# Cutting the last weight load of a decode kernel into five pieces instead of four

## The chip, the cores and the metric

One core of one Trainium2 chip. The metric is device time in microseconds (us). Before the change the kernel takes 1273.3 us (median of 3 runs, 1273.01 to 1273.58). Beside the time each run records the span of the core, about 2 us shorter.

## The reference, cut to what matters

A gated mix of a decode attention block and a small dense block. Two batch rows, one new token, 8 key/value heads, 32768 cached positions of 256 values, all bf16.

```python
def reference(A_x, A_k_cache, A_v_cache, A_wq, A_wo, B_x, B_w1, B_b1, B_w2, B_b2, gate_w):
    x = A_x                                             # [2, 1, 448]
    g = _sigmoid((x * gate_w).sum(-1, keepdims=True))
    a = _A_ref(x, A_k_cache, A_v_cache, A_wq, A_wo)     # softmax(q k) v, then @ wo [4096, 448]
    b = _B_ref(x, B_w1, B_b1, B_w2, B_b2)               # gelu(x w1 + b1) w2 + b2
    return g * a + (1 - g) * b
```

The two caches are 537 MB; each byte is used once. `wo` is 3.7 MB and is the last thing to be loaded.

## The kernel before

A ring of three buffers streams K and V. At the end of the queue of loads stand, in this order, the last V (three pieces), W2 and WO, all on one queue of the sync engine (SP). WO is laid out with 32 column blocks of 448 values in each of 128 partitions; a block is 112 KB. `WOP` says where WO is cut; each piece has its own semaphore.

```python
    NC = HD // P                          # 32 column blocks
    WOP = (0, 16, 28, 31, 32)             # pieces of 16, 12, 3 and 1 blocks
    ...                                   # --- cut ---
                elif kind == "WO":        # sync engine, L378 to L383
                    src = A_wo.rearrange("(p c) n -> p (c n)", p=P)
                    for i in range(len(WOP) - 1):
                        c0, c1 = WOP[i] * Dm, WOP[i + 1] * Dm
                        dma(lambda e, ...: e.dma_start(wo_v[:, c0:c1], src[:, c0:c1]), f"pW{i}", ("wo", i))
    ...                                   # --- cut ---
            def FIN(i):                   # TensorE: the product with WO, L551
                E.wait(f"pW{i}", ("wo", i))
                for c in range(WOP[i], WOP[i + 1]):
                    for q in range(2):
                        E.ins(lambda e, c=c, q=q: e.matmul(
                            ps_a[64 * q:64 * q + Bn, :], attnT[:, c:Bn * NC:NC],
                            wo_v[:, c * Dm + q * DQ:c * Dm + (q + 1) * DQ], ...))
    ...                                   # --- cut: the end of TensorE's program ---
            TT()
            do_FB()                       # the product with W2, 28 matmuls, L459
            E.wait("dve", "at")
            for i in range(len(WOP) - 1):
                FIN(i)                    # two matmuls a block, 64 in all
```

After the last matmul VectorE and ScalarE each cast one half of the result (L793, L656), and SP stores it (L396).

Of the kernel before, what the change touches and what calls it, by code (L numbers as in the profile page):

```python
# [125 lines left out]
def bass_gated_mix__gqa_block_cached__dense_activation_gelu__decode_kernel(  # L126
# [53 lines left out]
    assert (NTILES - LAG) % UNIT == 0  # L180
    PIECES = (64, 32, 32)
    NC = HD // P
    WOP = (0, 16, 28, 31, 32)
    DQ = Dm // 2
    GELU_C = 0.7978845608028654
    GELU_A = 0.044715
# [7 lines left out]
    for i in range(len(PIECES)):  # L194
        sch.stream(f"pV{i}", 16)
    for i in range(len(WOP) - 1):
        sch.stream(f"pW{i}", 16)
# [3 lines left out]
    with contextlib.ExitStack() as es:  # L201
# [157 lines left out]
        def prog_sp(E):  # L359
            def dma(fn, stream, key):  # L360
                E.ins(fn, key=key, stream=stream)

            for d in order:
# [15 lines left out]
                elif kind == "WO":  # L379
# [3 lines that stand above are left out]
                        dma(lambda e, src=src, c0=c0, c1=c1: e.dma_start(wo_v[:, c0:c1], src[:, c0:c1]), f"pW{i}", ("wo", i))  # L383
# [15 lines left out]
        def prog_pe(E):  # L399
# [147 lines left out]
            def FIN(i):  # L547
# [5 lines that stand above are left out]
                            wo_v[:, c * Dm + q * DQ:c * Dm + (q + 1) * DQ], start=False, stop=(c == NC - 1),  # L553
                            skip_group_check=True), key=("FIN" if (c == NC - 1 and q == 1) else None))
# [39 lines left out]
            E.wait("dve", "at")  # L594
            for i in range(len(WOP) - 1):
                FIN(i)
# [245 lines left out]
```

## Time and profile before

| what | value | where |
|---|---|---|
| span of the core | 1271.6 us | page |
| DMA busy | 90% or more in 39 of 40 slices, 431 GB/s | page |
| TensorE (PE), VectorE (DVE) busy | 55%, 54% | page |
| last WO piece landed | 1268.97 us | semaphore records of the trace |
| PE's last matmul ends | 1269.60 us | trace |

Lines of the page of the kernel before: span; busy time of the engines; the DMA share in 40 slices, in tenths; the chain of work that ended last, by engine.

```profile
span 1271.6 us, 8088 instructions
...
PE 698.9 (55%) x4544; PEld 146.0 (11%) x2016; DVE 685.8 (54%) x528; ACT 43.7 (3%) x183; POOL 3.3 (0%) x14
...
DMA  9999999999999999999999999999999999999998
...
DMA 63%; DVE 21%; PE 13%; issue 3%; SPq 0%; another core or an unknown queue 0%
```

The DMA row is 9 everywhere but in the last slice: the kernel is a stream. This change touches only the stream's very end, so what it can win lies there. That is the tail, from 1226 us. Here it is in the timeline of the kernel before. Columns: start (us), duration (us), engine, line, operation, destination <- source, shape, count, and in brackets the idle time before it and what ended it.

```profile
1226.42 1.84 SPq L383 DMA_DIRECT2D ring<-in_A_wo_dram  x4
...
1262.09 2.78 PE L459 MATMUL ps_f<-ring,hT_bf 128*2 128x224 bf16 x28
...
1264.76 2.14 PE L551 MATMUL ps_f<-ring,attnT 128*2 128x224 bf16 x32
...
1267.90 1.70 PE L551 MATMUL ps_f<-ring,attnT 128*2 128x224 bf16 x32 [1.00 <-DMA ring<-in_A_wo_dram]
...
1269.64 0.38 DVE L793 CAST pexp<-ps_f 2x224 bf16<-2x224 f32 x1 [7.21 <-PE ps_f L551]
```

SP issues the four WO loads by 1228.3 us, 40 us ahead. PE does the W2 product (28 matmuls), the 32 matmuls of piece 0, idles 1.00 us, and does all 32 others in one unbroken run of 1.70 us. The bracket names a WO load once: after piece 1 nothing made PE wait.

The issue table of the kernel before: size of each load, and us from its issue to its landing.

```profile
ring<-in_A_wo_dram SPq DMA_DIRECT2D x1, 1792.0 KB, 38.2
...
ring<-in_A_wo_dram SPq DMA_DIRECT2D x1, 1344.0 KB, 41.0
ring<-in_A_wo_dram SPq DMA_DIRECT2D x1, 336.0 KB, 41.3
ring<-in_A_wo_dram SPq DMA_DIRECT2D x1, 112.0 KB, 41.1
```

Issued at 1226.42, 1226.89, 1227.36 and 1227.83 us, they landed at 1264.6, 1267.9, 1268.7 and 1269.0. Twelve blocks took 3.2 us more, three 0.8, one 0.3: the DMA engine that finishes last brings a block about every 0.27 us (16 blocks in 4.34 us). Stretches of 2 us of the kernel before show that the others finish sooner. Columns: stretch; its length; busy time and count of each engine; granted clock; DMA share; GB/s.

```profile
core 0: us, PE busy (x) PEld busy (x) DVE busy (x) ACT busy (x) POOL busy (x), PEclk, DMA share, GB/s
...
1264.00:1266.00 2.00, 2.00 (x28) 1.29 (x26) 0.00 (x0) 0.00 (x0) 0.00 (x0) 0.58 0.96 401
1266.00:1268.00 2.00, 1.00 (x24) 0.69 (x20) 0.00 (x0) 0.00 (x0) 0.00 (x0) 1.00 0.53 204
1268.00:1270.00 2.00, 1.60 (x32) 1.23 (x28) 0.36 (x1) 0.34 (x1) 0.00 (x0) 1.00 0.02 6
```

The DMA share falls to 0.53 and 0.02 while the slower engines work on. The clock, 0.5 for most of the tail, is full from 1265.7 us.

### The profile page before, as it was taken

The numbers are of one execution on the slowest core, as the hardware profiler recorded it, in microseconds if no ns is written. First come the engines' busy times: TensorE is split into PE (matmuls) and PEld (weight loads), VectorE is DVE, ScalarE is ACT, GpSimd is POOL, SyncE is SP. The second block draws the span as 40 slices with busy tenths as digits, with TensorE's granted clock in tenths as the row PEclk, the third lists the DMA queues.
The fourth block names the chain that finished last, engine by engine and source line by source line (L and its number), as shares of the span: only waits on it lengthen the run. The fifth ranks groups of instructions, "written<-read, shape, count | busy, mean of one in ns | idle before, by whom it ended". The sixth has DMA issues, their size and how long they took to land.

```text
span 1271.6 us, 8088 instructions
## 1 busy us (share of the span) xinstructions
PE 698.9 (55%) x4544; PEld 146.0 (11%) x2016; DVE 685.8 (54%) x528; ACT 43.7 (3%) x183; POOL 3.3 (0%) x14
## 2 busy tenths in 40 slices
PE   4566566644466443665544665455664437655465
PEld 3111011100011100111100111000110001111012
DVE  2875537655365563556735466453755636566341
ACT  1000000000000000000000000000000000000000
POOL 1000000000000000000000000000000000000000
PEclk9988788767887777887778887778876778877686
DMA  9999999999999999999999999999999999999998
GB/s 404 441 434 431 429 429 435 431 439 434 431 429 435 437 431 437 435 431 429 433 439 431 437 435 429 431 433 439 431 437 433 431 431 433 439 431 433 437 423 359
DMA packets 10971, 547.59 MB, mean 431 GB/s; under 512 B 1352, under 2 KB 1616, under 8 KB 1872
## 3 DMA queue, kind: packets, MB, share of 16 engines
q1 hardware_dynamic: 10804, 547.43, 99.6%
q8 instruction: 8, 0.13, 0.0%
q10 hardware_dynamic: 156, 0.01, 0.0%
q14 instruction: 3, 0.02, 0.0%
HBM read 547.43 MB, written 0.00 MB: 431 GB/s over the span
## 4 chain that ended last, share of the span: by engine, by line
DMA 63%; DVE 21%; PE 13%; issue 3%; SPq 0%; another core or an unknown queue 0%
DMA ring<-in_A_k_cache_dram 60%; DVE ring L722 19%; PE ps_o L335 4%; PE ps_s L490 3%; PE ps_s L335 3%; DMA ring<-in_A_wo_dram 3%; DVE mx L726 1%; PE ps_o L539 1%; PE ps_m L499 0%; PE ps_m L504 0%; DVE gmax L728 0%; DVE gmx L732 0%; PE ps_f L551 0%; SPq L376 0%
## 5 line engine op out<-in xcount | busy, mean ns | idle before, releaser
L722 DVE STREAM_TRANSPOSE ring<-ring 128x2048 uint32<-128x2048 uint32 x256 | 565.2, 2275 | 390.2 <-DMA ring<-in_A_k_cache_dram 389.9
L490 PE MATMUL ps_s<-ring,Abd 128*128 128x512 bf16 x1024 | 427.0, 417 | 428.7 <-DVE ring L722 428.3
L335 PE MATMUL ps_s<-ring,Abd 128*128 128x512 bf16 x1024 | 423.3, 413 | 0.0
L490 PEld LDWEIGHTS ps_s<-ring,Abd 128*128 128x128 bf16 x1024 | 106.1, 104 | 852.0 <-DVE ring L722 480.1
L335 PE MATMUL ps_o<-ring,PT 128*24 128x512 bf16 x1504 | 112.9, 408 | 0.0
L539 PE MATMUL ps_o<-ring,PT 128*24 128x512 bf16 x544 | 58.1, 427 | 12.6 <-DMA ring<-in_A_v_cache_dram 12.6
L509 PE MATMUL ps_f<-o_sb,selg 128*32 128x257 f32 x32 | 17.0, 634 | 83.5 <-DVE o_sb L763 83.5
L763 DVE SCALAR_TENSOR_TENSOR o_sb<-ps_o,mask,o_sb 128x256 f32<-128x256 f32 x112 | 54.1, 483 | 8.9 <-PE ps_o L539 5.0
L726 DVE TENSOR_REDUCE mx<-ps_s 128x1 f32<-128x1024 f32 x16 | 19.6, 1224 | 59.9 <-PE ps_s L335 59.9
L636 ACT ACTIVATE negm<-ps_m 128x1 f32<-128x1 f32 x16 | 2.7, 171 | 1156.4 <-PE ps_m L504 1156.4
L739 DVE STREAM_TRANSPOSE PT<-pexp 128x1024 bf16<-128x1024 bf16 x16 | 19.9, 1245 | 36.8 <-PE ps_o L335 36.8
L539 PEld LDWEIGHTS ps_o<-ring,PT 128*24 128x24 bf16 x544 | 14.7, 100 | 104.1 <-issue 86.9
L736 DVE COPY ls<-lsum 128x1 f32<-128x1 f32 x16 | 2.5, 154 | 31.8 <-ACT pexp L640 31.8
L630 ACT COPY Abd<-qrep 32x16 bf16 (+1 forms) x128 | 19.4, 199 | 0.6
L640 ACT ACTIVATE pexp<-ps_s,negm 128x1024 bf16<-128x1024 f32 x16 | 17.8, 1113 | 1.7
L499 PE MATMUL ps_m<-ident_f,mx 128*1 128x128 f32 x32 | 6.1, 271 | 21.1 <-DVE mx L726 21.1
L760 DVE TENSOR_SCALAR o_sb<-ps_o,mask 128x256 f32<-128x256 f32 x16 | 7.6, 475 | 17.7 <-PE ps_o L335 17.7
L509 PEld LDWEIGHTS ps_f<-o_sb,selg 128*32 128x32 f32 x32 | 2.9, 139 | 101.6 <-DVE o_sb L763 99.5
L504 PE MATMUL ps_m<-ones_f,gmx 1*128 1x1 f32 x32 | 6.0, 256 | 9.9 <-DVE gmx L732 9.9
L728 DVE TENSOR_REDUCE gmax<-ps_m 1x2 f32<-1x128 f32 x16 | 4.5, 279 | 7.5 <-PE ps_m L499 7.5
L420 PE MATMUL ps_s<-xT,ring 128*128 128x2 bf16 x128 | 3.6, 165 | 8.1 <-DMA ring<-in_A_wq_dram 8.1
L504 PEld LDWEIGHTS ps_m<-ones_f,gmx 1*128 1x128 f32 x32 | 4.7, 183 | 14.6 <-DVE gmx L732 14.6
(76 smaller groups left out, 64.1 us busy)
## 6 DMA issues: line engine op xcount, KB each, us to landing
ring<-in_A_v_cache_dram SPq DMA_DIRECT2D x1, 4096.0 KB, 27.0
ring<-in_A_v_cache_dram SPq DMA_DIRECT2D x2, 2048.0 KB, 33.7
ring<-in_A_wq_dram SPq DMA_DIRECT2D x1, 3072.0 KB, 10.5
ring<-in_A_wo_dram SPq DMA_DIRECT2D x1, 1792.0 KB, 38.2
ring<-in_B_w_dram SPq DMA_DIRECT2D x1, 1568.0 KB, 34.3
ring<-in_B_w_dram SPq DMA_DIRECT2D x1, 1344.0 KB, 13.6
ring<-in_A_wo_dram SPq DMA_DIRECT2D x1, 1344.0 KB, 41.0
ring<-in_A_wq_dram SPq DMA_DIRECT2D x1, 512.0 KB, 11.3
```

What stands on the lines that cost most here:

```text
L335: return e.add_instruction(mybir.InstMatmult(name=f"I-{nc.next_id()}", engine=mybir.EngineType.PE, ldweights=False, ins=[e.lower_ap(x), e. ...
L490: fn = lambda e, o=o, x=x, st=st, sp=sp, s=s, w=w: e.matmul(o, a_win(s, w), x, start=st, stop=sp, skip_group_check=True)
L504: E.ins(lambda e: e.matmul(ps_m[:, C_BC:C_BC + 1], gmx[:, :], ones_f[0:1, 0:1], start=True, stop=True), key=("M2", g))
L509: E.ins(lambda e: e.matmul(ps_oa, selg[:, :], o_sb[:, :], start=False, stop=False, skip_group_check=True), key=("OT", g))
L539: fn = lambda e, o=o, x=x, wt=wt, st=st, sp=sp, j=j: e.matmul(o, wt, x, start=st, stop=sp, skip_group_check=True)
L630: E.ins(lambda e, o=o, Q=Q, c=c: e.copy(o[:, :, c:c + 2], qrep[32 * Q:32 * Q + 32, :, bass.ds(E.dyn(2 * g, 2), 2)]), key=(("A", g) if (Q = ...
L640: E.ins(lambda e: e.activation(pexp[:, :].rearrange("p (r i a) -> p i r a", r=CR, i=2), ps_s[:, :].rearrange("p (i r a) -> p i r a", i=2, ...
L722: E.ins(lambda e: e.transpose(k_words(idx, blk), k_words(idx, blk)), key=("T", idx, blk))
L726: E.ins(lambda e: e.tensor_reduce(mx[:, :], ps_s[:, :], AX.X, ALU.max), key=("MX", g))
L739: E.ins(lambda e: e.transpose(PT[:, :], pexp[:, :]), key=("PT", g))
L760: E.ins(lambda e, p=p, m=m: e.tensor_scalar(o_sb[:, 0:Dh], p, m, None, op0=ALU.mult), key=("OS0", g))
L763: E.ins(lambda e, p=p, m=m: e.scalar_tensor_tensor(out=o_sb[:, 0:Dh], in0=p, scalar=m, in1=o_sb[:, 0:Dh], op0=ALU.mult, op1=ALU.add), key= ...
```

## The change

The intent: less work for PE behind the last landings. A cut at 14, 23 and 28 instead of 16 and 28 lets PE finish 14 more matmuls before block 28 is there.

```diff
-    WOP = (0, 16, 28, 31, 32)
+    WOP = (0, 14, 23, 28, 31, 32)
```

It adds one DMA, one semaphore and one wait.

## The prediction

> **What bounds the kernel now.** The page of the profile: the 16 DMA engines are 90% busy or more in 39 of 40 slices, 547 MB at 431 GB/s over 1271.6 us; PE is busy 55%, DVE 54%. The chain of waits is 63% DMA. The change touches only the last loads, so only the tail after 1226 us can move.
>
> **The tail now** (timeline and chain of waits from 1220 us). The four WO loads are issued at about 1226.4, 1226.9, 1227.4 and 1227.8 us, behind a backlog of about 40 us, so issuing costs nothing. By the issue table they land 38.2, 41.0, 41.3 and 41.1 us later: about 1264.6, 1267.85, 1268.7 and 1268.95. The differences (12 column blocks in 3.25 us, 3 in 0.8, 1 in 0.27) say that the DMA engine that finishes last brings a block in about 0.27 us. Most engines are done earlier: by stretch, the DMA share falls from 1.0 at 1264 to 0.33 at 1267-1268 and 0.04 at 1268-1269.
> PE ends the W2 product at about 1264.7 and does the 32 matmuls of piece 0 by 1266.9, at a clock that goes from 0.50 to 1.00 near 1265.6. It idles 1.0 us for piece 1, until 1267.9. Then 32 matmuls (24, 6, 2) follow without a gap, 1.70 us, to 1269.62. So pieces 2 and 3 have landed before PE asks for them: behind the landing of block 28, PE is the limit, not the DMA. Only two casts (0.38 us) and the store follow.
>
> **What the change does.** It removes nothing: same bytes, same 64 WO matmuls, same engines. It adds one DMA issue on SP (0.43 us, hidden by the backlog), one semaphore, one wait on PE, and one more completion per DMA engine. With 0.27 us per block[...]:
> - piece 0 (14 blocks) lands at about 1264.1, before PE ends W2: no wait; 28 matmuls end near 1266.5.
> - piece 1 (to block 23) at about 1266.5: hardly a wait; 18 matmuls, done by 1267.4 at full clock.
> - piece 2 (to 28) at about 1267.9, as now: 10 matmuls, done by 1268.45.
> - piece 3 (to 31) at about 1268.7: now a real wait of about 0.3 us; 6 matmuls, 0.3 us.
> - piece 4 at about 1269.0: 2 matmuls; the end at 1269.3.
> So 14 matmuls less lie behind block 28's landing, and the limit becomes the landing of the last block. Of the 14 x 0.045 = 0.65 us moved off, about 0.3 us is gain; the rest becomes waiting for pieces 3 and 4. On 1273 us that is 0.02%, less than the spread of three runs (0.57 us).
>
> The Trainium skill, "DMA: Bandwidth & Descriptors", section "Anatomy of one DMA", gives a fixed cost of about 2 us per DMA that is mostly completion latency; in this trace queued pieces land 0.27 us apart, so it overlaps and must not be charged again.
>
> **Time:** 1273.0 us, 8 in 10 between 1271.9 and 1274.2. Faster by over 2%: 0.3%; within 2%: 99.4%; slower by over 2%: 0.3%.
>
> **What would show it.** All before 1226 us unchanged. PE's idle in front of the WO product in more, shorter parts; after the last landing 2 to 4 matmuls instead of some 20; the end about 0.3 us earlier relative to the last landing.
>
> **What would make it wrong.** If the half clock lasts through the tail, a matmul costs about 0.085 us and the gain is gone. If the slowest engine loses over 0.3 us to the extra piece, it is slower by some tenths. If runs differ by 0.1% anyway, only the trace shows the sign.

## The result, and the profile after

| | before | after |
|---|---|---|
| time, median (6 runs each) | 1273.10 us | 1272.85 us |
| lowest to highest | 1272.99 to 1273.58 | 1272.63 to 1273.11 |
| W2 landed to last WO landed (trace) | 8.64 us | 8.63 us |
| last WO landed to PE's end (trace) | 0.63 us | 0.33 us |
| W2 landed to PE's end (trace) | 9.26 us | 8.96 us |

The ratio is 0.9998, with a 95% interval of 0.9985 to 1.001. A ratio here is the mean time of one kernel's fast runs over that of the other's of the same rounds, so not quite the ratio of the medians. The verdict is "same". The time lies inside the predicted range, but so does the time of the kernel before (1273.10): a change that did nothing would have been in it too. The range does not test the mechanism; only the traces do.

The page of the kernel after, the lines that answer to those of before:

```profile
span 1270.7 us, 8089 instructions
...
PE 701.6 (55%) x4544; PEld 146.4 (12%) x2016; DVE 685.8 (54%) x528; ACT 43.7 (3%) x183; POOL 3.3 (0%) x14
...
DMA  9999999999999999999999999999999999999998
...
DMA 63%; DVE 19%; PE 15%; issue 3%; SPq 0%; another core or an unknown queue 0%
```

The span is 0.9 us shorter, and that is more than the change did. The W2 load, which the change leaves alone, landed 0.58 us earlier in this profile (1259.75 against 1260.33); I come back to why. I therefore measure the tail from W2's landing. Of the kernel before there is one profile; e5_front below, which has the same cuts from block 16 on, ends 9.34 us behind W2. The timeline of the kernel after:

```profile
1261.51 2.77 PE L459 MATMUL ps_f<-ring,hT_bf 128*2 128x224 bf16 x28
...
1264.08 1.64 PE L551 MATMUL ps_f<-ring,attnT 128*2 128x224 bf16 x28
...
1265.99 1.03 PE L551 MATMUL ps_f<-ring,attnT 128*2 128x224 bf16 x18 [0.27 <-DMA ring<-in_A_wo_dram]
...
1267.34 0.65 PE L551 MATMUL ps_f<-ring,attnT 128*2 128x224 bf16 x10 [0.32 <-DMA ring<-in_A_wo_dram]
1268.16 0.34 PEld L551 LDWEIGHTS ps_f<-ring,attnT 128*2 128x2 bf16 x8 [0.45 <-DMA ring<-in_A_wo_dram]
1268.16 0.55 PE L551 MATMUL ps_f<-ring,attnT 128*2 128x224 bf16 x8 [0.18 <-DMA ring<-in_A_wo_dram]
...
1268.76 0.38 DVE L793 CAST pexp<-ps_f 2x224 bf16<-2x224 f32 x1 [6.92 <-PE ps_f L551]
```

The unbroken run of 32 matmuls is gone. Piece 1 (18), piece 2 (10), and pieces 3 and 4 together (8) each come after a wait: the brackets name a WO load three times, for 0.27 and 0.32 us of matmul idle and 0.45 us of weight-load idle ahead of the last. Behind the last of these waits stand 8 matmuls, 0.55 us.

The issue table of the kernel after:

```profile
ring<-in_A_wo_dram SPq DMA_DIRECT2D x1, 1568.0 KB, 37.7
ring<-in_A_wo_dram SPq DMA_DIRECT2D x1, 1008.0 KB, 39.7
ring<-in_A_wo_dram SPq DMA_DIRECT2D x1, 560.0 KB, 40.5
ring<-in_A_wo_dram SPq DMA_DIRECT2D x1, 336.0 KB, 40.9
ring<-in_A_wo_dram SPq DMA_DIRECT2D x1, 112.0 KB, 40.7
```

Stretches of the kernel after:

```profile
1264.00:1266.00 2.00, 1.73 (x34) 1.25 (x32) 0.00 (x0) 0.00 (x0) 0.00 (x0) 0.91 1.00 411
1266.00:1268.00 2.00, 1.66 (x28) 1.05 (x28) 0.00 (x0) 0.00 (x0) 0.00 (x0) 1.00 0.53 203
1268.00:1270.00 2.00, 0.55 (x8) 0.27 (x8) 0.38 (x1) 0.34 (x1) 0.00 (x0) 1.00 0.04 9
```

The stream ends as before (DMA share 0.53, then 0.04), but from 1268 to 1270 PE has 8 matmuls left instead of 32. The clock is full a little earlier here (0.91 against 0.58 in the first stretch). All 16 engine landings of each piece are in the trace's semaphore records. Against the prediction, with the 0.58 us of W2 added to the profile's times:

| | predicted | measured + 0.58 |
|---|---|---|
| pieces 0, 1, 2 landed | 1264.1, 1266.5, 1267.9 | 1264.10, 1266.52, 1267.87 |
| pieces 3, 4 landed | 1268.7, 1269.0 | 1268.70, 1268.96 |
| PE's end | 1269.3 | 1269.29 |

One thing was not as predicted. The issues on SP of the kernel after (columns: count, shortest, median and longest in ns):

```profile
L383 SPq DMA_DIRECT2D ring<-in_A_wo_dram x5: 420/433/10564, 1225.8 to 1227.7; - x5
```

The fifth issue took 10.6 us, not 0.43. It ended at 1238.3 us, with 26 us to spare.

### The profile page after: what moved, and what is told of

Its sections match the earlier page's. It is cut to its first block, busy times and chain, and to the rows that moved or that the text cites. A ratio compares the mean times of both kernels' runs of the same rounds, so it can differ in the third digit from the quotient of the medians.

```text
span 1270.7 us, 8089 instructions
## 1 busy us (share of the span) xinstructions
PE 701.6 (55%) x4544; PEld 146.4 (12%) x2016; DVE 685.8 (54%) x528; ACT 43.7 (3%) x183; POOL 3.3 (0%) x14
## 4 chain that ended last, share of the span: by engine, by line
DMA 63%; DVE 19%; PE 15%; issue 3%; SPq 0%; another core or an unknown queue 0%
DMA ring<-in_A_k_cache_dram 59%; DVE ring L722 17%; PE ps_s L490 5%; PE ps_s L335 4%; PE ps_o L335 4%; DMA ring<-in_A_wo_dram 3%; DVE mx L726 1%; PE ps_o L539 1%; PE ps_m L504 0%; PE ps_m L499 0%; DVE gmax L728 0%; DVE gmx L732 0%; SPq L383 0%; SPq L376 0%
## 5 line engine op out<-in xcount | busy, mean ns | idle before, releaser
L335 PE MATMUL ps_o<-ring,PT 128*24 128x512 bf16 x1504 | 115.4, 415 | 0.0
L539 PE MATMUL ps_o<-ring,PT 128*24 128x512 bf16 x544 | 58.9, 432 | 14.0 <-DMA ring<-in_A_v_cache_dram 14.0
```

The costliest lines, as they stand in the source:

```text
L335: return e.add_instruction(mybir.InstMatmult(name=f"I-{nc.next_id()}", engine=mybir.EngineType.PE, ldweights=False, ins=[e.lower_ap(x), e. ...
L539: fn = lambda e, o=o, x=x, wt=wt, st=st, sp=sp, j=j: e.matmul(o, wt, x, start=st, stop=sp, skip_group_check=True)
```

## The experiments

Theory T says: PE ends when the last landings are in and the matmuls that stand behind them are done; the change moves 14 of them ahead. Rival N: all of it is scatter. Rival D: each piece costs DMA time, so fewer are better. Rival C: the fifth piece as such is what counts. Theory H, formed later, is about the clock.

Two remarks on the records quoted below. Where they say "the last V landing", it is in truth the landing of the second of the three last V pieces (1251.67 us in the profile before). All runs are measured alike, so differences stand. And in the tables I use W2's landing, the last event that the edits do not touch. "Mean span" is that of a kernel's five runs less that of the nine of before.

| run | pieces of WO | W2 to last landing | last landing to PE's end | W2 to PE's end | clock full from | mean span, less before |
|---|---|---|---|---|---|---|
| before | 16, 12, 3, 1 | 8.64 | 0.63 | 9.26 | 1265.70 | - |
| after | 14, 9, 5, 3, 1 | 8.63 | 0.33 | 8.96 | 1264.35 | - |
| e1_again | 14, 9, 5, 3, 1 | 8.66 | 0.34 | 9.00 | 1266.78 | -0.01 |
| e10_again | 14, 9, 5, 3, 1 | 8.68 | 0.33 | 9.01 | 1265.82 | -0.21 |
| e2_two | 16, 16 | 8.56 | 1.74 | 10.30 | 1267.03 | +1.25 |
| e3_one | 32 | 8.49 | 5.09 | 13.58 | 1272.11 | +4.49 |
| e4_each | 32 of 1 | 10.86 | 0.31 | 11.16 | 1267.27 | +2.11 |
| e5_front | 8, 8, 12, 3, 1 | 8.69 | 0.64 | 9.34 | 1265.15 | +0.08 |
| e6_four20 | 20, 8, 3, 1 | 8.63 | 0.31 | 8.93 | 1264.94 | +0.50 |
| e7_split120 | as e6, 4 blocks split by rows | 9.65 | 1.16 | 10.81 | 1269.56 | +1.50 |
| e8_fill20 | as e6, hole filled | 8.64 | 0.39 | 9.04 | 1265.91 | +0.21 |
| e9_hole5 | 20, 4, 4, 3, 1 | 8.67 | 2.41 | 11.08 | 1270.38 | +0.85 |
| e11_pairs | 16 of 2 | 9.36 | 0.40 | 9.76 | 1265.90 | +0.84 |

All times in us; columns 3 to 6 are of one profiled execution, the last is of five runs.

### e1_again: the changed kernel, more runs

No edit.

> The changed kernel once more (5 pieces of 14, 9, 5, 3, 1), for a better mean. Theory T (leftover matmuls): what PE still has to do behind the landing of column block 28 sets the end; 18 matmuls in place of 32, of which the later landings give back half. It expects 0.3 us less than before (0.28 by a sum of landings and matmuls), so a ratio of 0.9998, and in the trace about 0.3 us from the last load's landing to PE's end in place of 0.6 us. Rival N (nothing but scatter): the two kernels are equal in the mean and the 0.25 us of the first comparison is the scatter of runs; it expects a difference within 0.1 us of zero over the 5 rounds.

Median 1273.20 us, before 1273.22; ratio 1.0001 (0.9987 to 1.0015). The time speaks for N, the trace for T: 0.34 us from the last landing to PE's end, as in the first profile. Its timeline:

```profile
1264.36 4.66 PE L551 MATMUL ps_f<-ring,attnT 128*2 128x224 bf16 x64
1268.47 0.34 PEld L551 LDWEIGHTS ps_f<-ring,attnT 128*2 128x2 bf16 x8 [0.34 <-DMA ring<-in_A_wo_dram]
```

The clock came 2.4 us later than in the first profile (1266.78 against 1264.35), so 56 matmuls ran on with hardly a gap, and yet PE had caught up by the last wait. That also settles a rival: in the first profile the clock was full earlier than in the kernel before (4.60 against 5.37 us behind W2), but here it was later (6.76 us) and the gain is the same. The scatter of before in this call, 1272.91 to 1274.31, is larger than the gain sought. Only larger differences can decide by time, hence the next three.

### e2_two and e3_one: more work behind the last landing

```diff
-    WOP = (0, 14, 23, 28, 31, 32)
+    WOP = (0, 16, 32)          # e2_two;  e3_one: (0, 32)
```

> WO in two pieces of 16 and 16 blocks: the first as before, the last three merged. Theory T: all 32 last matmuls stand behind the last landing, so the end is 1.1 us later than before at full clock and 2.3 us later if the clock falls back to half in the 2 us of waiting. Rival N: within 0.2 us of before. Rival D (each piece costs DMA time, so that fewer are better): two pieces less save about 0.13 us, so it is 0.1 us faster than before.

> WO in one piece: 64 matmuls behind the last landing. Theory T: 2.5 us slower than before at full clock, 5.1 us at half clock; PE idles some 4 us ahead of them, so the clock may well be half for the first 3 us or so: I expect 3 to 5 us. Rival N: within 0.2 us. Rival D: 0.2 us faster than before.

e2: median 1274.26 us, 1.04 more than before. e3: 1277.58 us, 4.36 more. Timelines of e2, then of e3:

```profile
1268.76 1.70 PE L551 MATMUL ps_f<-ring,attnT 128*2 128x224 bf16 x32 [1.30 <-DMA ring<-in_A_wo_dram]
```

```profile
1268.54 4.95 PE L551 MATMUL ps_f<-ring,attnT 128*2 128x224 bf16 x64 [4.08 <-DMA ring<-in_A_wo_dram]
```

In e2 32 matmuls at full clock stand behind the last landing and take 1.70 us; in e3 64 take 4.95, mostly at the half clock, which lasted to 1272.11 us. T put the two at 1.1 and 3 to 5 us. N expected nothing, D a gain of 0.1 to 0.2. The 95% interval leaves out a ratio of 1 only for e3 (1.002 to 1.0047) and e4 (1.0002 to 1.0029). For e2 I go by the spans, which do not overlap: 1272.2 to 1272.7 against 1271.0 to 1271.6 before. N and D as whole explanations fall here. D is right in its small part: the stream itself is 8.64 us from W2 with four pieces, 8.56 with two and 8.49 with one, about 0.05 us a piece. That is rough: three profiles of the changed kernel alone differ by 0.05 (8.63 to 8.68).

### e4_each: the finest cut

```diff
+    WOP = tuple(range(33))
```

> WO in 32 pieces of one block, the finest split: leftover work is least. Theory T without any cost of a piece: 0.28 us faster than before, no better than the 5 pieces, as both then end with the landing of the last block. Rival D: a row of 896 bytes takes 41 ns by the packet records, 8 rows and a completion of 9 ns per engine and piece make 0.337 us a block, against 0.272 in large pieces; 28 pieces more than before should bring the last landing 1.8 us later and the end about 1.5 us later than before. T with that cost also expects plus 1.5 us, so this run measures the cost of a piece; beside it the sync engine may stall in issuing (the fifth WO issue took 10.6 us in the profile of the changed kernel), which would add gaps between the landings if it issues too late.

Median 1275.25 us, 2.03 more than before; W2 to PE's end is 1.90 us more, not 1.5. The leftover work is least, 0.31 us from the last landing to PE's end, no better than the change's 0.33. The timeline of e4, its last two waits:

```profile
1269.41 0.08 PEld L551 LDWEIGHTS ps_f<-ring,attnT 128*2 128x2 bf16 x2 [0.22 <-DMA ring<-in_A_wo_dram]
...
1270.95 0.26 PE L551 MATMUL ps_f<-ring,attnT 128*2 128x224 bf16 x2 [1.28 <-DMA ring<-in_A_wo_dram]
```

The rest of the 1.90 has two parts. First, pieces cost: block 31 landed 9.32 us behind W2, where a single load would have brought it in 8.49 x 31/32 = 8.22; 1.10 us for the 30 pieces beyond the first, 0.037 each. Second, the last block landed 1.54 us behind block 31 instead of 0.30. The packet records around it:

```
queue  start us  took ns  bytes
instr  1268.787    961    16384
data   1269.734    111      896
data   1269.831    111      896
...
data   1270.394     86      896
```

A packet of the instruction queue, 16 KB, ran from 1268.79 to 1269.75, and the eight rows of the last block that come after everything else began then. The records do not name the engine. That the fetch held them up on the same engine is argued from this coincidence in one trace; that all five runs were slow alike (spans 1273.1 to 1273.5) fits it. SP's own line in e4:

```profile
1227.77 40.21 SPq L383 DMA_DIRECT2D ring<-in_A_wo_dram  x32
```

SP spent 40 us issuing 32 loads, and a load landed 4.8 us after its issue in the median, 40 in the change. It no longer ran ahead of the stream: over the last nine blocks the first of a load's 16 landings comes every 0.47 us, which is SP's issuing interval, so the DMA engines that were 2 us ahead now waited for SP.

### e5_front: five pieces, old tail

```diff
+    WOP = (0, 8, 16, 28, 31, 32)
```

> Five pieces as in the change, but the new cut lies in front: 8, 8, 12, 3, 1. So the count of DMAs, waits and instructions is that of the changed kernel and the matmuls behind block 28 are again 32, as before. Measured in the trace from the last V load's landing to PE's last matmul, which leaves out how far the slowest DMA engine lags (before 17.95 us, changed 17.64). Theory T: 17.95 within 0.05, equal to before; PE's end 0.65 us behind the last landing. Rival C (the fifth piece, an added DMA and semaphore, is what counts): 17.65, as in the changed kernel.

0.64 us from the last landing to PE's end, 17.99 us by the measure of the record (the profile before: 17.92; the record has 17.95 for it). Median 1273.33 us, before 1273.09. Timeline of e5:

```profile
1264.27 2.13 PE L551 MATMUL ps_f<-ring,attnT 128*2 128x224 bf16 x32
...
1267.57 1.70 PE L551 MATMUL ps_f<-ring,attnT 128*2 128x224 bf16 x32 [1.17 <-DMA ring<-in_A_wo_dram]
```

The unbroken 32 matmuls of the kernel before are back. C falls: a fifth piece that leaves the work behind block 28 alone wins nothing.

### e6_four20: four pieces, new tail

```diff
+    WOP = (0, 20, 28, 31, 32)
```

> Four pieces as before, but 20, 8, 3, 1: no DMA, wait or instruction more than before; 24 matmuls behind block 28 in place of 32. Theory T: by the sum of landings and matmuls the gain is all there, 0.28 us: 17.65 us from the last V landing to PE's end, 0.35 us from the last landing to PE's end. Rival C: 17.95, as before. In time both are near the scatter: T expects 0.3 us less than before.

The profile is what T said: 0.31 us, 17.60 by the record's measure. Timeline of e6:

```profile
1265.89 3.43 PE L551 MATMUL ps_f<-ring,attnT 128*2 128x224 bf16 x64 [0.96 <-DMA ring<-in_A_wo_dram]
...
1268.77 0.38 PEld L551 LDWEIGHTS ps_f<-ring,attnT 128*2 128x2 bf16 x8 [0.16 <-DMA ring<-in_A_wo_dram]
```

The time is not. Median 1273.82 us, 0.73 more than before, and the five spans are 1271.3, 1270.7, 1272.3, 1273.2 and 1270.8, where before's nine lie between 1270.9 and 1271.4. (The median of the times overstates it: it falls on the run whose span is 1270.8. The mean span, 0.50 us more, is the better figure.) Something that this one profile does not show costs up to 2 us in some runs. The first piece lands at 1265.75 us and PE is done with W2 earlier, so PE idles 0.96 us in front of it. The stretches of e6:

```profile
1264.00:1266.00 2.00, 1.04 (x14) 0.50 (x12) 0.00 (x0) 0.00 (x0) 0.00 (x0) 0.77 0.95 387
1266.00:1268.00 2.00, 2.00 (x42) 1.67 (x40) 0.00 (x0) 0.00 (x0) 0.00 (x0) 1.00 0.49 190
1268.00:1270.00 2.00, 1.32 (x24) 0.83 (x24) 0.38 (x1) 0.34 (x1) 0.00 (x0) 1.00 0.02 6
```

Here the clock had just become full when the hole began. The Trainium skill, "TensorE: Matmul & The Clock Gate", Part 1 on the clock gate, says that the clock is set by how busy PE was in a window of 3413 ns that runs freely, not aligned to the kernel. Clock records agree: in all thirteen profiles every stretch of one clock lasts a multiple of 3.413 us within 0.01 (3.41, 6.83, 10.24, ...), but for the first and last of a record, and the edges differ from run to run. That gave theory H: a hole in PE's work that falls in the wrong window leaves the clock at half for another one or two.

### e7_split120: unequal shares for the DMA engines

```diff
-  dma(wo_v[:, c0:c1] <- src[:, c0:c1])
+  for p0, p1 in ((120, 128), (0, 120)):     # only for the last 4 blocks; pieces 20, 8, 3, 1
+      dma(wo_v[p0:p1, c0:c1] <- src[p0:p1, c0:c1])
```

> A probe of what bounds the tail once the leftover matmuls are gone: as the run with 20, 8, 3, 1, but the last two pieces (4 blocks) are each two DMAs, rows 120 to 127 and rows 0 to 119. If a DMA of 120 rows is dealt over 15 engines, one engine gets none of it and keeps only what the 8-row DMA may give it. The traces so far say that one engine lands everything last, 0.2 to 0.6 us behind the next. If that is the engine left out, the last landing comes earlier by that gap (17.2 to 17.4 us from the last V landing to PE's end in place of 17.65); if it is another, later by two extra pieces and a larger share, 0.05 to 0.2 us (17.7 to 17.85).

Both branches missed: 19.47 us, the median time 1.69 more than before. Two things came together. The last landing came 1.0 us later (9.65 from W2), because rows moved slower: of the 128 rows of 7168 bytes 43 took 286 to 494 ns, in e6 all took 272 to 284. These rows are piece 1, which is not split: it landed 8.74 us behind W2, in e6 7.51, so the delay was there before the split loads landed. I did not find out what made it. And the clock was half until 1269.56:

```profile
1265.23 5.32 PE L556 MATMUL ps_f<-ring,attnT 128*2 128x224 bf16 x64 [0.94 <-DMA ring<-in_A_wo_dram]
```

The split itself was as the Trainium skill has it ("DMA: Bandwidth & Descriptors", "Why a DMA increments its semaphore by 16 and not by 1"): 120 rows go to 15 engines, 8 rows to 8, and SP writes the missing increments itself. The trace agrees: the semaphore of piece 2 shows 25 updates, 23 (15 + 8) from 1265.6 us on and two at 1228.98 and 1229.41, each within 0.2 us of the end of one of the two issues. But as a way to a faster tail this is a failure, and which engine is the slowest stays unknown.

### e8_fill20 and e9_hole5: the hole, filled and added

e8 is e6 with 12 matmuls into scratch PSUM, read by nobody, between W2 and WO. e9 is the change with its first cut moved.

```diff
+    fill()        # e8: 12 x matmul(ps_s <- hT_bf, w2_v), start=True, stop=True; WOP = (0, 20, 28, 31, 32)
     for i in range(len(WOP) - 1):
         FIN(i)

+    WOP = (0, 20, 24, 28, 31, 32)      # e9
```

> The run with 20, 8, 3, 1 scattered over 2.5 us (spans of the core 1270.7 to 1273.2, before 1270.9 to 1271.6), although its profiled run was as expected. Theory H (the hole): with 20 blocks in the first piece PE idles about 1 us between the W2 product and it, and the TensorE clock, which changes only at ends of stretches of 3.41 us whose place differs from run to run, then stays at half in some runs, until late in the tail. Here 12 matmuls of 224 columns into scratch PSUM, whose result nothing reads, fill the hole (about 1 us at half clock); the DMAs stay as in that run. H expects the scatter gone (spans within 0.6 us of each other) and a mean span of 1270.7 to 1271.1, against 1271.17 before. Rival S (these piece sizes make the landings themselves erratic): the scatter stays above 1.5 us.

> The five pieces of the change with the first cut moved from 14 to 20: 20, 4, 4, 3, 1, so that the hole in front of the first piece is there with all else as in the change. H: the scatter is that of 20, 8, 3, 1 (spans over 1 us or more, mean 0.3 to 1 us above before), though not one matmul more stands behind block 28. If it is the count of pieces that steadies the changed kernel: spans within 0.6 us and a mean of 1270.9.

e9: median 1274.08 us, before 1273.13; spans 1273.1, 1272.9, 1270.8, 1272.1, 1270.9. The scatter of e6 is back, with five pieces and no more matmuls behind block 28 than in the change. Its profile caught a bad run. Timeline and stretches of e9:

```profile
1261.75 2.77 PE L459 MATMUL ps_f<-ring,hT_bf 128*2 128x224 bf16 x28
...
1265.47 5.60 PE L551 MATMUL ps_f<-ring,attnT 128*2 128x224 bf16 x64 [0.95 <-DMA ring<-in_A_wo_dram]
```

```profile
1264.00:1266.00 2.00, 1.05 (x14) 0.47 (x12) 0.00 (x0) 0.00 (x0) 0.00 (x0) 0.50 0.92 365
1266.00:1268.00 2.00, 2.00 (x26) 1.46 (x22) 0.00 (x0) 0.00 (x0) 0.00 (x0) 0.50 0.62 238
1268.00:1270.00 2.00, 2.00 (x26) 1.43 (x22) 0.00 (x0) 0.00 (x0) 0.00 (x0) 0.50 0.04 10
```

After W2 PE idles 0.95 us, and then 64 matmuls take 5.60 us, at clock 0.5 through all three stretches; the clock became full at 1270.38, and PE ended 2.41 us behind the last landing. This is H, seen.

The traces let H be tested window by window: cut each record into windows of 3.413 us at the clock's edges, and take PE's busy share of each. In all thirteen profiles the window before the tail's rise was 97% busy or more. In e9 the window from 1263.55 to 1266.96 holds the hole: 72% busy, and the clock stayed at half for one more window. In e7 it was the same (1262.74 to 1266.15, 73%). In e6's profile the hole began at the edge of 1264.94, with the clock just raised, and a window of 72% left it full; so did the window of 71% in the kernel before that holds its 1.00 us idle. So, in these traces, a hole costs when it falls in the window that would have raised the clock, not when the clock is already full. Of e6's own slow runs there is no profile.

e8: median 1273.42 us; spans 1270.8, 1271.9, 1271.4, 1270.9, 1271.6. Timeline of e8:

```profile
1264.07 1.33 PE L466 MATMUL ps_s<-ring,hT_bf 128*2 128x224 bf16 x12
...
1265.22 3.56 PE L558 MATMUL ps_f<-ring,attnT 128*2 128x224 bf16 x64
```

The excursions to 1272.3 and 1273.2 are gone (five runs, highest 1271.9), so S, which asked for a scatter above 1.5 us, falls, but H's own numbers were not met: 1.1 us between the spans instead of 0.6, a mean of 1271.32 instead of at most 1271.1. The likely reason is that the filling itself has to be done first: 40 matmuls of piece 0 begin behind it, and where the clock comes late they are not finished in time. That is an inference; no profile of a late run of e8 was taken.

### e10_again: the changed kernel on another chip

No edit.

> The changed kernel a third time, for its mean on another chip. So far its spans are 1270.88 in the mean (6 runs) and 1271.18 (5 runs), before 1271.17 (18 runs of two other calls). T expects 0.3 us less than before of the same call, give or take 0.1; if it is within 0.1 of before again, part of the gain that the profiles show is lost to something that they do not.

Median 1272.73 us, before 1273.13; mean span 0.21 us less, which is the lower end of T's 0.3 give or take 0.1. Pooled, the changed kernel's 16 spans have a mean of 1270.98 us (standard error 0.06), the 36 of before 1271.13 (0.03): 0.15 us. The three traces of the changed kernel say 0.25 to 0.30 (8.96, 9.00 and 9.01 against 9.26).

### e11_pairs: the cost of a piece

```diff
+    WOP = tuple(range(0, 33, 2))
```

> WO in 16 pieces of two blocks, to separate the two costs that the run with 32 pieces showed together: the last V landing to the landing of block 31 took 18.02 us there, which makes about 0.04 us for each piece beyond one (0.065 was my estimate from packet times), and the very last landing came 1.54 us behind it, 0.3 being due, as an instruction fetch of 16 KB sat on one DMA engine just then. With 0.04 us a piece, 16 pieces have the last landing 17.15 + 15 x 0.04 = 17.75 us behind the last V landing, and PE ends 0.3 to 0.4 us later, with 4 matmuls left: 18.1, so 0.15 us slower than before, if no fetch falls on the last block; about 1 us slower if one does. If a piece costs 0.065, 18.5 and plus 0.5 without a fetch.

Median 1273.86 us, 0.68 more than before. 18.53 us by the record's measure, the case "0.065 a piece, no fetch"; from W2's landing it is (9.36 - 8.49) / 15 = 0.058 us a piece. With e2 to e5 (about 0.05) and e4 (0.037) a piece costs 0.04 to 0.06 us in a full queue. Why it is less with 32 pieces is not settled.

## Why the prediction was right

- **What bounds the kernel** was right: the end of the stream, 8.64 us behind W2, is the same with and without the change (8.63 to 8.68).
- **Where PE is the limit** was right: 32 matmuls without a wait in e5 and before, 0.63 us behind the last landing; 0.33 with 18. e2 and e3 scale with the work left behind the landing, as T says.
- **The landings** were right within 0.04 us, once W2's landing is taken as zero.
- **The waits** were right in kind, more and shorter ones, but not in size: 0.27 us in front of piece 1 ("hardly a wait"), 0.32 in front of piece 2 (0.5 by the predicted times), 0.18 in front of piece 3 (0.3). That PE's end still fits within 0.01 us is partly luck.
- **"The limit becomes the landing of the last block"** was wrong by one piece. Piece 4 makes no wait of its own, because it lands while the 6 matmuls of piece 3 run. PE's end hangs on the landing of piece 3 (block 31) and the 8 matmuls behind it, 0.59 us. And "some 20" matmuls behind the last landing before were 8 that had not begun, 14 that had not ended; after, 2 and 8.
- **The size of the gain**, 0.3 us, is what the traces show (0.25 to 0.30). In time it is 0.25 us by the first medians and 0.15 us in the pooled spans; the two later calls that ran both kernels gave 0.01 and 0.21 us. So the gain in time is likely, but not shown as firmly as the gain in the traces. The missing 0.1 is not explained; it is about twice the standard error of the spans' difference (0.065), and may be chance.
- **"All before 1226 us unchanged"** failed as a test, though not by the change. In the profile after, everything before was 0.6 us earlier. The trace shows where such shifts come from. A load has 16 landings, one for each DMA engine. In the profile before the last of them came 0.69 us behind the second-last in a load at 192 us, and still 0.58 in one at 1252; in the profile after 0.38 and 0.19. So the lag of the last engine comes about early: from 308 us on it creeps from 0.47 to 0.65 in the profile before, and stays at about 0.23 in the profile after. It differs from run to run, and it is what moves W2's landing: over the thirteen profiles the second-last of W2's 16 landings lies between 1259.52 and 1259.81, the last between 1259.66 and 1260.39. That is as much as the gain and more. What makes it was not tested.
- **"One DMA issue on SP (0.43 us)"** was mis-sized: 10.6 us. It cost nothing only because SP was 40 us ahead. In e4 that lead was used up. This is the one cost that the prediction had wrong by a large factor.
- **"If the half clock lasts through the tail the gain is gone"** named a real danger, but not its cause. In e1 the clock came 2.4 us later and the gain stood (a matmul starts every 0.093 us at half clock and every 0.048 at full, where the prediction took 0.045). What keeps the clock at half is a hole in PE's work before the clock has risen (seen in e9 and e7, argued for e6), and the change's first cut at 14 happens to avoid it: piece 0 lands at 1263.52 us, before PE begins with WO at 1264.08. Judged by landings and matmuls alone, e6 would have been the better version, with one load fewer; it is slower by half a microsecond in the mean.

No experiment points to a version that beats the change. The leftover 0.33 us is the smallest measured but for 0.31 in e4 and e6, which lose elsewhere. What remains is the 2 us between the first and the last DMA engine, which e7 tried to use and made worse.

## What to carry to other kernels

Where a load stream ends a kernel, count the work that stands behind each of its last landings; cutting the load is worth at most that work less the wait for the next landing, here 0.3 of 1273 us. Choose the first cut so that the consumer has no hole in front of it: a hole of 1 us before the clock had risen cost up to 2 us, and only in some runs, so one good profile does not clear a version. Measure so small an effect from an event that the edit leaves alone, not in the span.

## What the Trainium skill lacked or had wrong

- "DMA: Bandwidth & Descriptors", "Anatomy of one DMA" and "Rules for kernel authors", give about 2 us of fixed cost per DMA and advise 1 MiB or more. In a full queue a further piece costs 0.04 to 0.06 us here, and small pieces at the end pay: 12, 3 and 1 blocks (1344, 336 and 112 KB) in place of 16 are 1.25 us better in the mean span (before against e2). The wait between the last data packet and the last semaphore update is 0.43 us in the profile before (1268.53 to 1268.97), a fraction of those 2 us. (The page measured another issue path; this kernel issues from SP.)
- I found no page that says how far SP can issue ahead: the fifth WO load's issue took 10.6 us where the others took 0.43, and 32 loads took 40.2 us. In all seven profiles of kernels with five pieces or more the fifth took 8.8 to 10.6 us and ended between 1238.2 and 1238.6; in e7, with six loads, the sixth took 3.3.
- "TensorE: Matmul & The Clock Gate" warns of idle gaps of over some 3.4 us. Here a gap of 0.95 us was enough to keep the clock at half for one more window of 3.41 us (e9: to 1270.38 instead of 1266.96), when it fell in the window that would have raised it, which was then 72% busy.
- "Runtime: NRT & Kernel Launch", "Instruction fetch mechanics", says that instructions are fetched in 16 KiB blocks by DMA and that the cost is mostly hidden. The blocks show in the trace (16384 bytes, 0.96 us in one packet); in e4 the last load landed 1.24 us late beside one, which is a coincidence in one trace and not shown to be the cause.
- No page that I read says that the lag of the last DMA engine behind the second-last can arise early and stay to the end, and that it differs from run to run: at W2's landing it is 0.65 us in the profile before, 0.23 in the profile after and 0.02 in e10_again.
